# Retention and two expert layers on one core: state products ahead of scores times values, weight sets ahead of conversions, stores begun in the attention

## The chip, the cores and the metric

The kernel runs on one core of a Trainium2 chip. The metric is the device time in microseconds of one execution; of several runs the median counts. The core's engines are TensorE (PE, with its weight loads as PEld), VectorE (DVE), ScalarE (ACT), GpSimd (POOL) and SyncE (SP), which issues nearly all DMAs.

## What is computed

```python
# q, k, v: (4, 8, 768, 64); retention with a decaying state, head by head
for t in range(S):
    state = gamma * state + einsum('bhd,bhe->bhde', k[:, :, t], v[:, :, t])
    y[:, :, t] = scale * einsum('bhd,bhde->bhe', q[:, :, t], state)
x = y.transpose(0, 2, 1, 3).reshape(3072, 512)
h = x @ moe_w_in;  x = maximum(0.01 * h, h) @ moe_w_out     # 512 -> 2048 -> 512
h = x @ moe2_w_in; x = (h - tanh(h)) @ moe2_w_out           # 512 -> 2048 -> 512
```

The weights come as 64-bit floats (two int32 words each) and are made into 32-bit floats on the chip.

## The kernel before

The kernel writes each engine's order out by hand: an instruction stands in its engine's queue where the Python code emits it, and an engine works its queue strictly in order.

**Attention.** The 768 positions are cut into six chunks c of 128, the eight heads into four pairs p. A step s is one (c, p) for all four batches; 24 steps, in the order c = 0, 1 for pair 0, then for pair 1, and so on, so that steps 0, 2, 4, 6 are of chunk 0 and steps 17, 19, 21, 23 of chunk 5. A step runs, on TensorE, the transposes of the next step's k (`a_Tk`, kTp, L515) and of half of a q (`a_Tq`, qTp, L529), the output y (`a_Y`): U times q (L573, not for chunk 0, which has no state yet) and masked scores A times v (L577), then the state product u = k times v (`a_U`, L596, not for chunk 5), then the next step's scores sc (`a_S`, L550). VectorE masks the scores into A (L554) and adds u to the state U (L600); ScalarE scales k (L494), copies kT (L517), qT (L530) and the three pieces of y into x (L581, and L583 twice), and for chunk 0 copies u (L598); GpSimd scales q (L506). SP loads k, q, v for step s + 4 in step s (L447, L458).

**Background work in the attention.** After each step from `CONV_FROM` on, `run` emits some 2.3 us (`ATT_US`) of VectorE work from two queues, taking the second where the first has nothing to give. `conv` is the conversion of the 16 column blocks of moe_w_in: a raw block of 512 KB is loaded (L202, three blocks ahead), then ScalarE does one operation (L208) and VectorE four (L212, L214, L217, L220). `bg` makes what the products need: `build_xc`, the activations of the first two chunks split into a high part on ScalarE (xch, L174) and a low part on VectorE (xcl, L180), with differences between them (L385); and `build_wg(g)`, a weight set from two converted blocks: high parts wg on ScalarE (L174, L176), sums s (L327, L329, L335, L337) and low parts wg (L180, L182) on VectorE. In even steps `bg` comes first, in odd ones `conv`.

**Products.** Behind the attention TensorE runs moe_w_in in a form with seven products (P1 to P7) for each set g and each pair of chunks sb; a product is six matmuls (L768). VectorE adds pairs of results (L781), ScalarE copies (L775) and rectifies (L757), SP stores g1s (L758). The rest of the sets and conversions, and of the activations, is emitted between the products. The first 12 products use sets 0 and 1 alone. In the same place SP stores the 16 outputs x of chunks 2 to 5 to x1s, one behind each product (L829). They are loaded again later as the next activations.

Of the kernel before, what the change touches and what calls it, by code (L numbers as in the profile page):

```python
# [14 lines left out]
AF = mybir.ActivationFunctionType  # L15
# [4 lines left out]
P = 128  # L20
NB, NH, NS, ND = 4, 8, 768, 64
DM, DFF = 512, 2048
NC = NS // P
NPAIR = NH // 2
# [14 lines left out]


N_ATT, N_FFN = 64, 94
CONV_FROM, ATT_US = 5, 2.3

LOAD_LEAD = 5
KV_BUFS = 6
# [29 lines left out]
def kernel(  # L75
# [12 lines left out]
    nc = tc.nc  # L88
# [12 lines left out]
    x1s = dr.tile([NC, NK, P, TB], F32, tag="x1s", name="x1s")  # L101
# [10 lines left out]
    def alloc(nm, dt=F32, shape=(P, TB)):  # L112
        pool, tag = free.popleft()
        serial[0] += 1
        t = pool.tile(list(shape), dt, tag=tag, name=f"{nm}_{serial[0]}")
        home[id(t)] = (t, pool, tag)
        return t

    def give(*ts):
        for t in ts:  # L120
            _, pool, tag = home.pop(id(t))
            free.append((pool, tag))
# [5 lines left out]
    def run(queues, us):  # L128

        while us > 0:  # L130
            for queue in queues:
                cost = next(queue[0], "end") if queue else None
                if cost is not None:
                    break
            if cost is None:
                return 0.0
            if cost == "end":
                queue.popleft()
            else:
                us -= cost  # L140
        return us
# [171 lines left out]
    def build_wg(g):  # L313
        while g + NG not in UN or g not in UN or len(free) < 10:
            yield None
        yield from form_sets(UN.pop(g), UN.pop(g + NG), lambda w, ts: WG.update({g: (w, ts)}))
# [104 lines left out]
            done()  # L421

    xw = {}

    def free_x():
        give(*(xw.pop((c, p)) for c in range(2) for p in range(NPAIR)))


    with tc.tile_pool(name="at", bufs=2, reuse_waits="tile") as at, \
            tc.tile_pool(name="atp", bufs=1, space=PSUM, reuse_waits="tile") as atp:  # L430
        steps = [(c, p) for cc in range(0, NC, 2) for p in range(NPAIR) for c in (cc, cc + 1)]
        S = {}

        def a_load(s):
            if s >= len(steps):
                return
            c, p = steps[s]
            load_kv(s, "k", k)
            if c % 2:
                a_load_q(s + 1)  # L440
            load_kv(s, "v", v)
# [91 lines left out]
        def a_T(s):  # L533
            a_Tk(s)
            if s % 2:
                a_Tq(s + 1, 0)
            else:
                a_Tq(s, 2)

        def a_S(s):  # L540
            if s >= len(steps):
                return
            c, p = steps[s]
            d = S[s]
            tq = slice(c % 2 * P, (c % 2 + 1) * P)
            sc = [atp.tile([P, NB, P], F32, tag=f"sc{h}", name=f"sc_{s}_{h}") for h in range(2)]
            for b in range(NB):
                for h in range(2):
                    r = slice(h * ND, (h + 1) * ND)
                    nc.tensor.matmul(sc[h][:, b, :], d["kT"][r, b, :], d["qT"][r, b, tq], start=True, stop=True)  # L550
            d["A"] = []
            for h in range(2):
                a = at.tile([P, NB, P], F32, tag=f"A{h}", name=f"A_{s}_{h}", bufs=1)
                nc.vector.scalar_tensor_tensor(out=a, in0=sc[h], scalar=_decay(2 * p + h) ** -float(P), in1=tri4,  # L554
                                               op0=ALU.mult, op1=ALU.mult)
                d["A"].append(a)

        def a_Y(s):
            c, p = steps[s]
            d = S[s]  # L560
            tq = slice(c % 2 * P, (c % 2 + 1) * P)
            half = (slice(0, ND), slice(ND, P))
            ys = [atp.tile([P, NB, P], F32, tag=f"y{i}", name=f"y_{s}_{i}") for i in range(2)]

            def place(b, h):
                i = b // 2
                return ys[i][half[h ^ i], b % 2, :]

            if c > 0:
                for b2 in range(2):  # L570
                    for b in (b2, b2 + 2):
                        for h in range(2):
                            nc.tensor.matmul(place(b, h), U[p][half[h], b, :], d["qT"][half[h], b, tq], start=b2 == 0,  # L573
                                             stop=False)
            for b in range(NB):
                for h in range(2):
                    nc.tensor.matmul(place(b, h), d["v"][:, b, h, :], d["A"][h][:, b, :], start=c == 0 and b % 2 == 0,  # L577
                                     stop=b % 2 == 1)
            xw[c, p] = x = alloc("x1")
            flat = [y.rearrange("p b t -> p (b t)")[:, :2 * P] for y in ys]  # L580
            nc.scalar.activation(out=x[:, :2 * P], in_=flat[0], func=AF.Copy)  # L581
            for h in range(2):
                nc.scalar.activation(out=x[half[h], 2 * P:], in_=flat[1][half[1 - h]], func=AF.Copy)  # L583
            if c == 1 and p == NPAIR - 1:
                XQ[0] = {nm: [xw[th, 2 * kh], xw[th, 2 * kh + 1]]
                         for nm, kh, th in (("B11", 0, 0), ("B21", 1, 0), ("B12", 0, 1), ("B22", 1, 1))}

        def a_U(s):
            c, p = steps[s]
            d = S[s]  # L590
            if c < NC - 1:
                u = atp.tile([P, NB, ND], F32, tag="u", name=f"u_{s}")
                for b in range(NB):
                    for h in range(2):
                        r = slice(h * ND, (h + 1) * ND)
                        nc.tensor.matmul(u[r, b, :], d["k"][:, b, h, :], d["v"][:, b, h, :], start=True, stop=True)  # L596
                if c == 0:
                    nc.scalar.activation(out=U[p], in_=u, func=AF.Copy)  # L598
                else:
                    nc.vector.scalar_tensor_tensor(out=U[p], in0=U[p], scalar=gc[:, p:p + 1], in1=u, op0=ALU.mult,  # L600
                                                   op1=ALU.add)
            if c % 2:
                del S[s - 1], S[s]

        conv = deque([conversion(conv_in)])
        bg = deque([build_xc(one, 0, 0), build_wg(0), build_xc(one, 0, 1), build_wg(1), build_xc(one, 0, 2, free_x)])
        us = 0.0
# [12 lines left out]
        for s in range(len(steps)):  # L620
            a_load(s + 4)
            a_scale_k(s + 2)
            if s % 2:
                a_scale_q(s + 3)
            if s == 0:
                a_Tk(1)
                a_Y(0)
                a_Tq(2, 0)
            else:
                a_T(s + 1)  # L630
                a_Y(s)
            a_U(s)
            a_S(s + 1)
            tick[0] += 3
            if s >= CONV_FROM:
                us = run((conv, bg) if s % 2 else (bg, conv), min(us + ATT_US, ATT_US))

# [25 lines left out]
    def upper_g(o):  # L665
        if o < 2 * NT:
            G[o] = alloc("gh", F32R), None
            upper(G[o][0], GR[o])
# [138 lines left out]
    bg.extend(build_wg(g) for g in range(2, NG))  # L807
    bx = deque(build_xc(one, sb, part) for sb in range(1, NSB) for part in range(3))
    loads = deque(load_xq(one, sb, lambda at=SPAN * (sb - 1) + 38: now[0] >= at) for sb in range(1, NSB))
    xleft = [(c, p) for c in range(2, NC) for p in range(NPAIR)]  # L810
    us = 0.0
    for i, (at_, sb, g, nm) in enumerate(stream):
        an, bn, bk, _ = PROD[nm]
        while g not in WG or bn not in XC.get(sb, {}):
            tick[0] += 1
            run((loads, bg, bx, conv), 0.01)
        product(sb, g, nm)
        now[0] = at_
        tick[0] += 1
        done, late[:] = late[:], []  # L820
        used = collect(sb, g, nm)
        for args in done:
            rectify(*args)
        if sb == NSB - 1 and nm == "P4":
            give(*WG[g][1])
        if xleft:
            c, p = xleft.pop(0)
            t = xw.pop((c, p))
            nc.sync.dma_start(out=x1s[c, p], in_=t)  # L829
            give(t)  # L830
        us = run((loads, conv, bg, bx) if not sb and at_ >= BG_FIRST and at_ % 2 == 0 else (loads, bg, bx, conv), min(us + SLOT_US - used, SLOT_US))
        if len(stream) - 11 <= i < len(stream) - 11 + G_AHEAD:
            load_g(i - len(stream) + 11)
        if len(stream) - 6 <= i < len(stream) - 3:
            upper_g(i - len(stream) + 6)
        if len(stream) - 5 <= i < len(stream) - 3:
            lower_g(i - len(stream) + 5)
        if i == len(stream) - 2:
            step(0)
# [71 lines left out]
    us = 0.0  # L911
    for n in range(ND_FROM):
# [16 lines left out]
        us = run((loads, bx, forms, conv), min(us + 2.0, 2.0))  # L929
# [195 lines left out]
    while i < NPROD or halves:  # L1125
# [11 lines left out]
        while halves and (i == NPROD or gone < i * n_mid / NPROD):  # L1137
            o, half = halves[0]
# [9 lines left out]
def _decay(h):  # L1148
    return 1.0 - 2.0 ** (-5.0 - h)
# [49 lines left out]
```

## Time and profile before

| | |
|---|---|
| median of 3 runs | 1058.73 us (1057.42 to 1059.09) |
| profiled execution, its own time | 1059.45 us |
| its span | 1057.7 us |
| PE busy | 1041.5 us (98%) |
| DVE, ACT busy | 826.7 us (78%), 721.1 us (68%) |
| chain that ended last | PE 89%, DVE 4%, DMA 3%, ACT 2% |
| granted TensorE clock | 1.0 of full speed, all through |

The attention takes the first 109 us, the first products follow. Busy time is an average over stages with different limits, so the stages are looked at one by one: which wait ends last there. Matmul ends are modelled, so a small gap of TensorE is seen better in its weight loads (PEld).

### The profile page before, as it was taken

To read this page: it belongs to the slowest core of one execution; us is meant where nothing else is said; L and a number is where in the kernel's file an instruction comes from. 1 tells how busy PE (TensorE), PEld (TensorE's weight loads), DVE (VectorE), ACT (ScalarE), POOL (GpSimd) and SP (SyncE) were. 2 spreads that over 40 slices of the span, in tenths; PEclk is the share of its full clock that TensorE was granted. 3 is DMA by queue.
4 is the path that set the end of the run, shared out by engine and by line. 5 is a ranking of instruction groups with operands and counts; after the bars stand their busy time and mean duration, and the time that the engine had idled before them with its cause. 6 is when DMAs were issued, how large, how long until landed. Compare 5 with 4: busy or idle time off the path is not lost.

```text
span 1057.7 us, 17635 instructions
## 1 busy us (share of the span) xinstructions
PE 1041.5 (98%) x5931; PEld 902.2 (85%) x5931; DVE 826.7 (78%) x1363; ACT 721.1 (68%) x1299; POOL 93.2 (9%) x124
## 2 busy tenths in 40 slices
PE   9999899999999999999999999999999999999998
PEld 6888778888888888888888888888888888888887
DVE  3589897774788999967999789898878988687630
ACT  6889676766776556656777679887668766666440
POOL 3232000000000000000110111001100110011000
PEclk9999999999999999999999999999999999999999
DMA  9998465675668899959999988998987988878641
GB/s 223 242 269 233 164 234 190 208 250 210 225 234 286 287 361 388 393 200 285 276 323 298 324 257 260 303 290 261 316 252 224 268 246 255 259 220 229 190 149 40
DMA packets 208634, 267.67 MB, mean 253 GB/s; under 512 B 65056, under 2 KB 106144, under 8 KB 208544
## 3 DMA queue, kind: packets, MB, share of 16 engines
q1 hardware_dynamic: 197888, 247.52, 70.1%
q0 software_dynamic: 10368, 18.88, 10.3%
q8 instruction: 47, 0.77, 0.3%
q14 instruction: 43, 0.35, 0.1%
q10 hardware_dynamic: 288, 0.15, 0.1%
HBM read 161.63 MB, written 85.98 MB: 234 GB/s over the span
## 4 chain that ended last, share of the span: by engine, by line
PE 89%; DVE 4%; DMA 3%; ACT 2%; issue 1%; SPq 0%; DVEq 0%; ACTq 0%
PE o L693 46%; PE Xd L1040 11%; PE X L768 9%; PE Yd L1040 6%; PE Y L768 4%; PE Zd L1040 3%; PE y L577 2%; PE sc L550 2%; PE Z L768 2%; PE kTp L515 1%; PE y L573 1%; PE qTp L529 1%; DVE c L781 1%; PE u L596 1%; DMA gr<-g1s 1%
## 5 line engine op out<-in xcount | busy, mean ns | idle before, releaser
L693 PE MATMUL o<-gh,wo 128*128 128x512 f32 x768 | 239.5, 379 | 0.0
L693 PEld LDWEIGHTS o<-gh,wo 128*128 128x128 f32 x768 | 145.2, 189 | 20.4
L174 ACT ACTIVATE gh<-gr 128x512 fp32r<-128x512 f32 x192 | 118.3, 621 | 54.1 <-DMA gr<-g1s 26.9
L180 DVE TENSOR_TENSOR gl<-gr,gh 128x512 fp32r<-128x512 f32 x192 | 130.1, 683 | 27.9 <-ACT gh L174 22.5
L693 PE MATMUL o<-gl,wo 128*128 128x512 f32 x384 | 145.9, 380 | 2.5 <-DVE gl L180 2.5
L693 PE MATMUL o<-w2h,gh 128*128 128x512 f32 x384 | 145.5, 379 | 0.0
L693 PE MATMUL o<-w2h,gl 128*128 128x512 f32 x384 | 145.5, 379 | 0.0
L693 PE MATMUL o<-w2l,gh 128*128 128x512 f32 x384 | 145.5, 379 | 0.0
L1020 POOL DMA_DIRECT2D et<-h x72 | 62.1, 862 | 826.9 <-DVE gl L180 424.3
L1040 PE MATMUL Xd<-xch,wf 128*128 128x512 f32 x384 | 129.5, 379 | 0.0
L768 PE MATMUL X<-xch,wg 128*128 128x512 f32 x384 | 123.2, 381 | 3.7 <-DVE wg L180 2.5
L1007 DVE COPY_PREDICATED es<-mk,et 128x512 f32<-128x512 uint16 x96 | 70.9, 742 | 44.6 <-ACT mk L981 44.6
L768 PEld LDWEIGHTS X<-xch,wg 128*128 128x128 f32 x384 | 72.4, 189 | 17.0 <-DVE wg L180 3.4
L693 PEld LDWEIGHTS o<-gl,wo 128*128 128x128 f32 x384 | 72.6, 189 | 14.3 <-DVE gl L180 4.1
L969 ACT ACTIVATE eu<-h 128x512 f32<-128x512 f32 x96 | 59.9, 624 | 33.3 <-DVE h L949 31.2
L693 PEld LDWEIGHTS o<-w2l,gh 128*128 128x128 f32 x384 | 72.6, 189 | 10.3
L693 PEld LDWEIGHTS o<-w2h,gh 128*128 128x128 f32 x384 | 72.6, 189 | 10.3
L1040 PEld LDWEIGHTS Xd<-xch,wf 128*128 128x128 f32 x384 | 72.6, 189 | 10.3
L693 PEld LDWEIGHTS o<-w2h,gl 128*128 128x128 f32 x384 | 72.6, 189 | 10.3
L1040 PE MATMUL Xd<-xcl,wf 128*128 128x512 f32 x192 | 72.8, 379 | 0.0
L768 PE MATMUL X<-xcl,wg 128*128 128x512 f32 x192 | 72.8, 379 | 0.0
L985 DVE SCALAR_TENSOR_TENSOR ew<-eu,h 128x512 f32<-128x512 f32 x96 | 65.5, 683 | 8.8 <-DMA wfs<-wg 3.2
(101 smaller groups left out, 2030.3 us busy)
## 6 DMA issues: line engine op xcount, KB each, us to landing
wf<-wfs SPq DMA_DIRECT2D x168, 256.0 KB, 4.3
g1s<-c SPq DMA_DIRECT2D x96, 256.0 KB, 2.2
gr<-g1s SPq DMA_DIRECT2D x96, 256.0 KB, 5.3
g2s<-es SPq DMA_DIRECT2D x96, 256.0 KB, 3.5
gr<-g2s SPq DMA_DIRECT2D x96, 256.0 KB, 4.2
et<-h POOLq DMA_DIRECT2D x72, 256.0 KB, 5.3
raw<-in_moe_w_in_dram SPq DMA_DIRECT2D x32, 512.0 KB, 5.7
raw<-in_moe_w_out_dram SPq DMA_DIRECT2D x32, 512.0 KB, 4.4
```

What stands on the lines that cost most here:

```text
L174: nc.scalar.activation(out=hi, in_=src, func=AF.Copy)
L180: nc.vector.tensor_tensor(out=lo, in0=src, in1=hi.bitcast(F32), op=ALU.subtract)
L515: nc.tensor.transpose(ps[:, b, :], d["k"][:, b].rearrange("p h d -> p (h d)"), ident)
L550: nc.tensor.matmul(sc[h][:, b, :], d["kT"][r, b, :], d["qT"][r, b, tq], start=True, stop=True)
L577: nc.tensor.matmul(place(b, h), d["v"][:, b, h, :], d["A"][h][:, b, :], start=c == 0 and b % 2 == 0, stop=b % 2 == 1)
L693: nc.tensor.matmul(ACC[j], a, il(b), start=first and i == 0, stop=last and i == 2)
L768: nc.tensor.matmul(ps, w[:, c], il(x), start=first and kt == 0 and i == 0, stop=kt == 1 and i == 2, skip_group_check=True)
L969: nc.scalar.activation(out=e["u"], in_=h, func=AF.Square)
L985: nc.vector.scalar_tensor_tensor(out=e["w"], in0=e["u"], scalar=C3, in1=h, op0=ALU.mult, op1=ALU.mult)
L1007: nc.vector.copy_predicated(out=e["s"], mask=e["mk"].bitcast(mybir.dt.uint16), data=e["th"])
L1020: nc.gpsimd.dma_start(out=e["th"], in_=h, accum_op=ALU.add)
L1040: nc.tensor.matmul(ps, a, il(b), start=nm in ("P1", "P2", "P5") and kt == 0 and j == 0, stop=kt == 1 and j == 2, skip_group_check=True)
```

## The change

It does five things. (1) `a_U` moves from behind `a_Y` into it: the state product u is emitted behind U times q and ahead of A times v (behind the transposes, where U times q is missing). (2) In steps 0 to 7 (`DVE_UNTIL` = 8) the two half copies of y are VectorE's. (3) Background work begins after step 2 instead of step 5. (4) `bg` comes first in every step. (5) From step 16 (`STORE_FROM`) on, each step stores one x, and the products the rest; `store_x` is the old code in a function.

```diff
-CONV_FROM, ATT_US = 5, 2.3
+CONV_FROM, ATT_US = 2, 2.3
+STORE_FROM, DVE_UNTIL = 16, 8
...
+    xleft = [(c, p) for c in range(2, NC) for p in range(NPAIR)]
+
+    def store_x():
+        if xleft:
+            c, p = xleft.pop(0)
+            t = xw.pop((c, p))
+            nc.sync.dma_start(out=x1s[c, p], in_=t)
+            give(t)
...
                             nc.tensor.matmul(place(b, h), U[p][half[h], b, :], d["qT"][half[h], b, tq], start=b2 == 0,
                                              stop=False)
+            a_U(s)
             for b in range(NB):
...
             for h in range(2):
-                nc.scalar.activation(out=x[half[h], 2 * P:], in_=flat[1][half[1 - h]], func=AF.Copy)
+                if s < DVE_UNTIL:
+                    nc.vector.tensor_copy(x[half[h], 2 * P:], flat[1][half[1 - h]])
+                else:
+                    nc.scalar.activation(out=x[half[h], 2 * P:], in_=flat[1][half[1 - h]], func=AF.Copy)
+            if c % 2:
+                del S[s - 1], S[s]
...
-            a_U(s)
             a_S(s + 1)
+            if s >= STORE_FROM:
+                store_x()
             tick[0] += 3
             if s >= CONV_FROM:
-                us = run((conv, bg) if s % 2 else (bg, conv), min(us + ATT_US, ATT_US))
+                us = run((bg, conv), min(us + ATT_US, ATT_US))
...
-        if xleft:
-            c, p = xleft.pop(0)
-            t = xw.pop((c, p))
-            nc.sync.dma_start(out=x1s[c, p], in_=t)
-            give(t)
+        store_x()
```

The emission follows the queues, so the order moves as well. VectorE, from the last A of the attention on (wg, xcl, s as above; cv is a block in conversion, c an addition of two products), before:

```order
L554 SCALAR_TENSOR_TENSOR A_1_1860<-sc_1_1849,cst 128x512
L180 TENSOR_TENSOR wg_1800<-cv_895,wg_1799 128x512
L335 TENSOR_TENSOR s_58_1798<-cv_895,cv_1048 128x256
L337 TENSOR_TENSOR s_58_1798<-cv_895,s_57_1797 128x256
L180 TENSOR_TENSOR wg_1802<-s_57_1797,wg_1801 128x512
L180 TENSOR_TENSOR wg_1804<-s_58_1798,wg_1803 128x512
L781 TENSOR_TENSOR c_1917<-Z_0_1910,P_68_1903 128x512
L182 SCALAR_TENSOR_TENSOR wg_1805<-cv_1048,wg_1805 128x256
L180 TENSOR_TENSOR xcl_1922<-x_6_557,xch_1921 128x512
```

and of the change (its lines are shifted: L563 is L554, L213 L212, L221 L220, L328 L327, L795 L781):

```order
L563 SCALAR_TENSOR_TENSOR A_1_1887<-sc_1_1876,cst 128x512
L213 TENSOR_SCALAR cv_1776<-cv_1776 128x512
L215 TENSOR_SCALAR cv_1776<-cv_1776 128x512
L218 SCALAR_TENSOR_TENSOR cv_1776<-raw_0_1236,cv_1776 128x512
L221 SCALAR_TENSOR_TENSOR cv_1776<-raw_0_1236,cv_1776 128x512
L213 TENSOR_SCALAR cv_1890<-cv_1890 128x512
L215 TENSOR_SCALAR cv_1890<-cv_1890 128x512
L218 SCALAR_TENSOR_TENSOR cv_1890<-raw_0_1774,cv_1890 128x512
L221 SCALAR_TENSOR_TENSOR cv_1890<-raw_0_1774,cv_1890 128x512
L328 TENSOR_TENSOR s_81_1945<-cv_1238 128x256
L330 TENSOR_TENSOR s_81_1945<-s_81_1945,cv_1001 128x256
L795 TENSOR_TENSOR c_1966<-Z_0_1959,P_80_1942 128x512
```

Before, the rest of weight set 1, six xcl and four differences still stand behind the last A, and eight of the 16 conversions of moe_w_in are done ahead of it. With the change none of these stands there, both sets and all activations of the first two chunks are made ahead of it, and six conversions are.

SP, around the first raw loads (k_591 is the k of step 10), before:

```order
L447 DMA k_510<-in_k_dram 128x4x64 x2
L458 DMA q_513<-in_q_dram 128x4x128 x2
L447 DMA v_516<-in_v_dram 128x4x64 x2
L202 DMA raw_0_585<-in_moe_w_in_dram 128x4x256
L202 DMA raw_0_587<-in_moe_w_in_dram 128x4x256
L202 DMA raw_0_589<-in_moe_w_in_dram 128x4x256
L447 DMA k_591<-in_k_dram 128x4x64 x2
L447 DMA v_594<-in_v_dram 128x4x64 x2
```

and of the change, where k_315 is that of step 6 and k_381 that of step 7:

```order
L456 DMA k_315<-in_k_dram 128x4x64 x2
L456 DMA v_318<-in_v_dram 128x4x64 x2
L203 DMA raw_0_375<-in_moe_w_in_dram 128x4x256
L203 DMA raw_0_377<-in_moe_w_in_dram 128x4x256
L203 DMA raw_0_379<-in_moe_w_in_dram 128x4x256
L456 DMA k_381<-in_k_dram 128x4x64 x2
L467 DMA q_384<-in_q_dram 128x4x128 x2
L456 DMA v_387<-in_v_dram 128x4x64 x2
```

The raw loads move ahead by three steps of k, q and v. Up to the last v of the attention SP then issues seven raw loads and three x1s stores, where it issued nine raw loads and no store.

ScalarE between two kT, in step 16 (chunk 4), before:

```order
L517 ACTIVATE kT_1389<-kTp_1384 128x512
L530 ACTIVATE qT_1391<-qTp_0_1392 128x2x2x128
L581 ACTIVATE x_44_1416<-y_0_1398 128x256
L583 ACTIVATE x_44_1416<-y_1_1399 64x256 x2
L174 ACTIVATE wg_1134<-s_30_1130 128x512
L208 ACTIVATE cv_1450<-raw_0_1293 128x512
L494 ACTIVATE k_1295<-k_1295,lead 128x4x64 x2
L517 ACTIVATE kT_1475<-kTp_1470 128x512
```

and of the change (L596 is L583, L175 L174, L177 L176):

```order
L526 ACTIVATE kT_1423<-kTp_1418 128x512
L539 ACTIVATE qT_1425<-qTp_0_1426 128x2x2x128
L591 ACTIVATE x_57_1460<-y_0_1432 128x256
L596 ACTIVATE x_57_1460<-y_1_1433 64x256 x2
L175 ACTIVATE wg_1323<-s_48_1318 128x512
L177 ACTIVATE wg_1325<-cv_830 128x256
L175 ACTIVATE xch_1484<-x_8_581 128x512
L175 ACTIVATE xch_1486<-x_11_726 128x512
L503 ACTIVATE k_1330<-k_1330,lead 128x4x64 x2
L526 ACTIVATE kT_1512<-kTp_1507 128x512
```

Two pieces of background work between y and the next kT have become four.

## Rows read from the trace of the kernel before

**Rows 1.** Attention, first products: PE, PEld, DVE, ACT, POOL busy (instructions); clock, DMA share, GB/s

```profile
13.00:109.00 96.00, 94.57 (x1548) 81.42 (x1548) 69.20 (x118) 81.20 (x182) 26.91 (x40) 1.00 0.92 236
109.00:165.00 56.00, 50.97 (x233) 42.50 (x230) 50.95 (x97) 40.29 (x73) 0.00 (x0) 1.00 0.55 197
```

**Rows 2.** Who TensorE waited for, 104 to 165 us: total, times, longest

```profile
PE X L768 <- DVE wg L180: 2.5, 2, 1.3
PE Y L768 <- DVE xcl L180: 1.7, 1, 1.7
...
PE Y L768 <- DVE wg L180: 0.4, 1, 0.4
```

**Rows 3.** VectorE by line and shape, 109 to 165 us: busy, mean ns, idle before

```profile
L180 DVE TENSOR_TENSOR wg<-s,wg 128x512 fp32r<-128x512 f32 x10 | 6.6, 693 | 2.8 <-ACT wg L174 2.8
...
L217 DVE SCALAR_TENSOR_TENSOR cv<-raw,cv 128x512 int32<-128x512 int32 x8 | 6.5, 807 | 0.2
...
L180 DVE TENSOR_TENSOR xcl<-x,xch 128x512 fp32r<-128x512 f32 x6 | 3.9, 684 | 1.5 <-ACT xch L174 1.5
...
L214 DVE TENSOR_SCALAR cv<-cv 128x512 int32<-128x512 int32 x8 | 3.4, 424 | 0.2
...
L385 DVE TENSOR_TENSOR x<-x,x 128x512 f32<-128x512 f32 x4 | 2.6, 682 | 0.0
...
L335 DVE TENSOR_TENSOR s<-cv,cv 128x256 f32<-128x256 f32 x5 | 2.1, 416 | 0.0
```

**Rows 4.** Two VectorE operations of 512 columns in a row

```profile
117.09 1.28 DVE L385 TENSOR_TENSOR x<-x,x 128x512 f32<-128x512 f32 x2
```

**Rows 5.** TensorE's weight loads in time order, steps 4 and 5: start, us, [idle]

```profile
28.56 0.74 PEld L577 LDWEIGHTS y<-A,v 128*64 128x64 f32 x13 [0.23 <-DVE A L554]
...
30.04 0.97 PEld L550 LDWEIGHTS sc<-qT,kT 64*128 64x128 f32 x16
...
34.24 0.97 PEld L550 LDWEIGHTS sc<-qT,kT 64*128 64x128 f32 x16
```

**Rows 6.** The same, the two steps in which TensorE waited for kT

```profile
47.04 0.97 PEld L550 LDWEIGHTS sc<-qT,kT 64*128 64x128 f32 x16 [0.45 <-ACT kT L517]
...
52.11 1.06 PEld L550 LDWEIGHTS sc<-qT,kT 64*128 64x128 f32 x16 [0.94 <-ACT kT L517]
```

**Rows 7.** ScalarE in time order: one early step, then the two steps of rows 6

```profile
30.77 0.90 ACT L494 ACTIVATE k<-k,lead 128x256 f32<-128x256 f32 x2
...
45.54 0.96 ACT L494 ACTIVATE k<-k,lead 128x256 f32<-128x256 f32 x2 [1.10 <-DMA k<-in_k_dram]
...
47.39 0.38 ACT L581 ACTIVATE x<-y 128x256 f32<-128x256 f32 x1
...
48.59 2.19 ACT L174 ACTIVATE xch<-x 128x512 fp32r<-128x512 f32 x4
...
51.48 0.57 ACT L517 ACTIVATE kT<-kTp 128x512 f32<-128x512 f32 x1
```

**Rows 8.** The first three raw loads: issue, and time to landing

```profile
L202 SPq DMA_DIRECT2D raw<-in_moe_w_in_dram x3: 617/694/722, 36.6 to 38.1; - x3
...
DMA to landing us min/median/max: 5.7/6.4/7.0
```

**Rows 9.** The k load right behind them

```profile
L447 SPq DMA_DIRECT2D k<-in_k_dram x2: 442/1062/1683, 38.8 to 39.3; - x2
...
DMA to landing us min/median/max: 6.7/6.7/6.7
```

**Rows 10.** The k load of step 7, with no raw ahead of it

```profile
L447 SPq DMA_DIRECT2D k<-in_k_dram x2: 440/472/505, 25.3 to 25.8; - x2
...
DMA to landing us min/median/max: 2.8/2.8/2.8
```

**Rows 11.** VectorE by line and shape in the attention, 13 to 109 us

```profile
L554 DVE SCALAR_TENSOR_TENSOR A<-sc,cst 128x512 f32<-128x512 f32 x46 | 29.6, 684 | 18.0 <-PE sc L550 17.9
L600 DVE SCALAR_TENSOR_TENSOR U<-U,lead,u 128x256 f32<-128x256 f32 x16 | 7.6, 475 | 9.6 <-PE u L596 9.6
```

More of the change, by code (lines that the diff above doesn't have):

```diff
@@ L601, in a_U @@
                                                    op1=ALU.add)
-            if c % 2:
-                del S[s - 1], S[s]
         conv = deque([conversion(conv_in)])
@@ L809 @@
     loads = deque(load_xq(one, sb, lambda at=SPAN * (sb - 1) + 38: now[0] >= at) for sb in range(1, NSB))
-    xleft = [(c, p) for c in range(2, NC) for p in range(NPAIR)]
     us = 0.0
```

## Prediction

> **What bounds the kernel now.** I read the windows by stage first, then who waits for whom on TensorE, then the engines it waits for. TensorE computes 94.57 of 96 us in the attention [rows 1], so a change gains there only through the order of its steps or a stall taken out. In the 56 us behind it TensorE loses 5.03 us while VectorE is busy 50.95 [rows 1]: VectorE is the bound there. The waits name the places [rows 2]: 2.5 + 0.4 us for weight sets (wg) and 1.7 us for one low part of the converted activations (xcl). These 4.6 us are the largest loss that the change can reach.
>
> In the attention the reader is to see three things. A step of the first chunk, which has no state-times-query products, waits 0.23 us for the masked scores A [rows 5]. Two steps wait 0.45 and 0.94 us for kT [rows 6]. And the reason for these is on ScalarE [rows 7]: it sat 1.10 us until a k load had landed, and in the next step it had four xch conversions (2.19 us) ahead of its next kT.
>
> **Products stage.** The order shows what leaves it. Behind the last A there were six xcl, four x differences (L385) and six operations of weight set 1; now there are none of these, but ten conversions instead of eight. By the durations [rows 3]: 6 x 0.684 + 4 x 0.682 + 3 x 0.693 + 3 x 0.416 = 10.2 us go; a conversion is 0.42 + 0.42 + 0.81 + 0.81 = 2.5 us (L220 taken like L217, L212 like L214), so two more cost 4.9. VectorE is relieved of 5.2 us.
>
> Does TensorE get it? A product is six matmuls of 50.97 / 233 = 0.219 us [rows 1], 1.31 us. Sets 0 and 1 carry the first 12 products, 15.7 us. Until set 2 is complete VectorE has two conversions (4.9), two additions (1.4), five 256-column and three 512-column operations (4.2): 10.5 us by durations. But operations in a row overlap: two of 0.68 take 1.28 [rows 4], one each 0.60, so 88%: 9.3 us, and 6.4 us of lead. Each later set comes every 7 products (9.2 us) and costs VectorE two conversions, one set and three additions: 4.9 + 4.2 + 2.0 = 11.1 us by durations, 9.8 with the overlap. Five sets eat 3.0 of the 6.4 us. So the wg and xcl waits go and I take **-4.6 us**. Bounds: -5.0 (all that TensorE loses there goes) and -1.7 (only the xcl wait goes, for that work is no longer there; the wg waits return, as they would by the durations without overlap, since 5 x 1.9 is more than 5.2).
>
> **States before values.** u moves between U-times-q and A-times-v; it adds no instruction and its inputs k and v have landed steps before. Where U-times-q is missing (steps 0, 2, 4, 6), u fills the 0.23 us for A [rows 5]: 4 x 0.23 = **-0.9 us**, between that and nothing. The other steps have the same products in another order: nothing. The price is that ScalarE's copies of y now start as the scores start, no longer behind u as well; that shortens the time that ScalarE has from one y to the next kT, see the last term.
>
> **Half of the copies to VectorE, steps 0 to 7.** 16 copies. The nearest row is U, also 256 columns from PSUM, 0.475 us [rows 11], 7.6 us in all. VectorE waited 17.9 us for scores and 9.6 us for u in the attention [rows 11], mostly in these steps; that hides them. Without this cover, in the two steps that also hold a conversion, A would come some 0.5 us late, and u in front of A-times-v gives that back. ScalarE loses the same copies. Taken as nothing, at most 1.0 the wrong way.
>
> **Conversion from step 2.** The first three raw loads now stand on SP ahead of the k of step 7 instead of step 10. This removes and adds a stall. Removed: the late k and, as the four xch now follow a step with one ScalarE copy less and no late k, the wait behind them: 0.45 + 0.94 [rows 6], **-1.4 us**. Added: the old k behind the raws was issued 2.2 us after the first of them and took 6.7 us [rows 8, 9]; k of step 7 took 2.8 from 25.3 us [rows 10]. Shifted by 2.2 + 3.9 it lands at 34.2; as SP's queue is emptier there, I take one us less, 33.2. ScalarE scaled it at 30.77 [rows 7]. TensorE's scores follow the scaling by 1.5 us (45.54 to 47.04, [rows 6, 7]), so 34.7; they stood at 34.24 [rows 5] and would stand at 33.55 with three shorter steps. That is 1.2 us, and the k of step 8 still some 0.7 late: **+1.9 us**. Bounds: 0.4, as before, and 4.2, all three raws at the 1.4 us between their landings (first 36.6 + 5.7, last 38.1 + 7.0, two between [rows 8]).
>
> How long the debt lasts decides much. The DMA engines show a share of 0.92 at 236 GB/s in the attention [rows 1]; read as room, that is a twelfth, and a debt of 4.2 us would last some 50 us (rival 2). The Trainium skill ("DMA: Bandwidth & Descriptors", section "Where 436 GB/s comes from") puts the limit of transfers from HBM at about 358 GB/s per core; by it 122 GB/s would be spare and the three raws (1.57 MB) caught up within an estimated 13 us, three steps. The trace before shows no stretch at that rate. I keep the sum at two late k because only one k came late behind the raws before [rows 7].
>
> **Weight sets ahead of conversion.** ScalarE's pieces pile up where they are not alternated: behind step 16 the order has four (two wg, two xch), at 2.19 / 4 = 0.55 us [rows 7] some 2.0 us, and the step that follows has no u. ScalarE is idle (96 - 81.2) / 24 = 0.62 us a step [rows 1]. So between nothing and 1.4 us; I take **+0.6 us**, nearer to the low end because k and kT come before qT.
>
> **Stores.** Eight of the 16 x1s stores go out from step 16 on, three of them ahead of the last loads, where the seven raws ahead of the last v were nine. Half a raw each, 0.7 us of the queue: 2.1 against 2.8 saved. Taken as nothing.
>
> **Sum.** -4.6 - 0.9 - 1.4 + 1.9 + 0.6 = -4.4 us. The profiled execution took 1059.45 us (span 1057.7 and 1.75 around it): 1055.05. The median of the runs is 0.72 below it, so I predict **1054.3 us**. With all terms at their good ends -5.0 - 0.9 - 1.4 + 0.4 = -6.9, at their bad ends -1.7 - 1.4 + 4.2 + 1.4 + 1.0 = +3.5.
>
> **Rival 1, the weight sets wait again.** VectorE works in order; its lead is spent while it waits for the product that an addition needs, and ten conversions remain. Then only the xcl wait goes: 2.9 us less gain, 1057.2 us. For it: without overlap sets 5 to 7 are late. Against: VectorE idles 5 us in that stage today, partly for ScalarE [rows 3], and set 2 now has 6 us of lead.
>
> **Rival 2, slower: the loads pace the attention.** If SP never regains the lead that the early raws cost, each transfer ahead of the last v delays the attention: seven raws at 1.4 and three stores at 0.7 are 11.9 us. -4.6 - 0.9 - 1.4 + 11.9 + 0.6 = +5.6: 1064.3 us. It decides from the point where k lands later than ScalarE wants it in step after step, beyond step 9. For it: the share of 0.92. Against: nine raws before cost 1.4 us of waiting only, and the k behind three of them came just 1.10 us late [rows 7].
>
> **How the numbers follow.** A measurement of this kernel tells 0.2% (2.1 us) from no change, so faster is below 1056.6. My forecast has a chance of 0.74 (1051.5 to 1056.6, from the good ends), rival 1 0.16 (no change), rival 2 0.10 (slower). The range leaves out rival 2 and the edges of the others: 1051.5 to 1057.6.
>
> **What would show it.** Right: no wait of TensorE for xcl or wg between the end of the attention and 165 us; a first product still near 109 us; ScalarE waiting some 2 to 3 us for the k of steps 7 and 8, and none later; step 16 half a us longer. Wrong: k waits beyond step 9, or wg waits over 1 us in all, or a gain that stands elsewhere than before 165 us.

## The result and the profile after

The change makes the kernel slower: 1064.96 us, the median of six runs (1064.46 to 1067.85), against 1058.72 us before (six runs), a ratio of 1.0066 with a 95% interval of 1.0053 to 1.0079. I had predicted 1054.3 us, so the forecast missed by 10.7 us and had the wrong sign. The profiled execution is the slowest of the six: 1067.85 us, span 1066.1 us. It stands 2.9 us above the median, and its terms below add up to more than the median shows.

The attention and the first products, in windows that meet near the first product, as in [rows 1] (same columns):

```profile
13.00:111.00 98.00, 94.25 (x1529) 79.30 (x1529) 78.88 (x142) 77.66 (x173) 26.36 (x40) 0.98 0.93 245
111.00:165.00 54.00, 53.53 (x255) 46.46 (x251) 49.97 (x94) 37.46 (x69) 0.00 (x0) 1.00 0.56 191
```

Who TensorE waited for (total, times, longest), from 104 to 165 us, where [rows 2] stood:

```profile
PE Y L782 <- ACT P L789: 0.5, 1, 0.5
PE y L587 <- DMA raw<-in_moe_w_in_dram: 0.2, 1, 0.2
PE y L587 <- DVE A L563: 0.2, 1, 0.2
```

and from 165 to 300 us, where the kernel before has one entry, 0.7 us for c:

```profile
PE Y L782 <- DVE xcl L181: 1.0, 4, 0.3
PE X L782 <- ACT xch L175: 0.9, 2, 0.4
PE X L782 <- DVE xcl L181: 0.8, 3, 0.3
PE X L782 <- DVE c L795: 0.7, 2, 0.3
PE Y L782 <- ACT xch L175: 0.5, 1, 0.5
PE Z L782 <- DVE xcl L181: 0.2, 1, 0.2
```

The reader is to see that the products do what was forecast: the waits for weight sets and for the first xcl are gone, and TensorE loses 0.5 us between 111 and 165 us. But waits of a kind that the profile before did not have stand behind 165 us, for the activations of the next chunks (xch, xcl). The clock of the attention is 0.98 of full speed; before, it was 1.00.

The sizes come from comparing the start of the same matmul in both traces, after minus before. Behind the first layer four more names occur: gl is the low part of a loaded result of the first layer, st a copy of finished output, kp ScalarE's copy of a product of the second layer, wf a weight set of the second layer as TensorE uses it.

| place | time before | change minus before | what happened since the line above |
|---|---|---|---|
| first product | 109.23 us | +2.26 us | attention |
| products, first pair of chunks, late | 161.97 | -3.67 | -5.9: no wait for wg, xcl |
| second pair of chunks, after its start | 203.50 | +0.13 | +3.8: xch, xcl |
| third pair, after its start | 276.64 | +2.53 | +2.4: xch, xcl |
| products with moe_w_out begin | 354.08 | +2.78 | +0.25 |
| moe_w_out and second layer mixed | 521.35 | -0.01 | -2.8: two gl waits of before (1.76 and 0.74 us) are not paid here |
| the same | 561.60 | +4.04 | +4.0: its own waits for st and gl |
| the same | 609.30 | +8.16 | +4.1: kp, st |

So the gain of the products was real, and it was gone by 203 us. That is where the experiments look.

### The profile page after: what moved, and what is told of

It is laid out like the page before. It is cut to its first block, busy times and chain, and to the rows that moved or that the text cites. A ratio compares the mean times of both kernels' runs of the same rounds, so it can differ in the third digit from the quotient of the medians.

```text
span 1066.1 us, 17641 instructions
## 1 busy us (share of the span) xinstructions
PE 1043.5 (98%) x5931; PEld 900.4 (84%) x5931; DVE 832.6 (78%) x1379; ACT 710.9 (67%) x1283; POOL 92.7 (9%) x124
## 4 chain that ended last, share of the span: by engine, by line
PE 88%; DVE 4%; DMA 4%; ACT 3%; issue 2%; SPq 0%; ACTq 0%; DVEq 0%; POOLq 0%; POOL 0%
PE o L707 44%; PE Xd L1049 11%; PE X L782 10%; PE Y L782 5%; PE Yd L1049 5%; PE Z L782 3%; PE Zd L1049 2%; PE sc L559 2%; PE y L587 2%; PE kTp L524 1%; DMA gr<-g1s 1%; PE u L611 1%; PE y L582 1%; PE qTp L538 1%; DVE xcl L181 1%
## 5 line engine op out<-in xcount | busy, mean ns | idle before, releaser
L175 ACT ACTIVATE gh<-gr 128x512 fp32r<-128x512 f32 x192 | 118.4, 623 | 62.3 <-DMA gr<-g1s 22.1
L1002 DVE SCALAR_TENSOR_TENSOR es<-es,ew 128x512 f32<-128x512 f32 x96 | 66.1, 688 | 4.0
```

The lines of the kernel that those rows point to most:

```text
L175: nc.scalar.activation(out=hi, in_=src, func=AF.Copy)
L1002: nc.vector.scalar_tensor_tensor(out=e["s"], in0=e["s"], scalar=K1, in1=e["w"], op0=ALU.add, op1=ALU.mult)
```

## The experiments

Each kernel was timed together with the kernel before on the same chip. The kernel before took 1060.4 us beside the kernels with later loads, with the old alternation, with the raws one a step from step 2 and with the states alone; 1060.0 us beside the repeat, the released loads, the start at step 5 and the copies on ScalarE; and 1059.9 us beside the two that combine edits. So ratios are given; the times in the expectations were written against 1058.7 us, in the two that combine edits against 1059.5. xq_B names the loads of the next activations from x1s, g1s the results that the products store.

**The changed kernel again** (no edit).

> The changed kernel itself, run again, for what of its profile repeats. If the losses belong to its order of work: a wait of about 2 us for the k of step 7 at 33 us, waits for xch and xcl at 184 and 262 us, a wait behind wf near 610 us; time 1064 to 1069 us. If the wait near 610 us was chance (the profiled execution was 2.9 us above the median), it is missing in this profile.

Measured: 1066.0 us, ratio 1.0058 (1.0046 to 1.0070). Its own profile, span 1063.2 us, repeats the structure: waits for xch and xcl at 182 to 191 and 261 to 266 us, and the one near 610 us, which is therefore not chance:

```profile
610.34 0.80 PE L1049 MATMUL Xd<-xch,wf 128*128 128x512 f32 x1 [3.02 <-ACT kp L951]
```

What does not repeat is the size of the wait for the k of step 7. It was 1.99 us in the first profile and 0.90 here, and the first products start 0.53 us later than before instead of 2.26. The load of q, which stands behind the raws as well, is late too, so that TensorE waits for the scaled q (qp):

```profile
33.84 1.23 PE L559 MATMUL sc<-qT,kT 64*128 64x128 f32 x16 [0.90 <-ACT kT L526]
36.35 1.01 PE L538 MATMUL qTp<-cst,qp 128*128 128x128 f32 x4 [0.69 <-POOL qp L515]
```

Two kernels below keep these loads as they are. With the activation loads released the wait at this place was 0.42 us and the first products started 1.00 us earlier than before; with all copies on ScalarE it was 2.21 us and they started 2.21 us later. One profile therefore says little about what an edit does to this stall.

**The kernel before with later loads of the activations.**

```diff
-    loads = deque(load_xq(one, sb, lambda at=SPAN * (sb - 1) + 38: now[0] >= at) for sb in range(1, NSB))
+    loads = deque(load_xq(one, sb, lambda at=SPAN * (sb - 1) + 42: now[0] >= at) for sb in range(1, NSB))
```

> The kernel before, with the loads of the next activations (xq_B) allowed four products later (42 instead of 38 products into each pair of chunks) and nothing else changed. Theory 1 (late loads of activations cost the changed kernel 3.8 + 2.4 us): waits of TensorE for xch and xcl appear at the start of the second and third pair of chunks, 2.5 to 4 us each, none before 165 us; the same gap opens in the second expert layer only if its order moves too. Total 1058.7 + 5 to 7 = 1064 to 1066 us. Theory 2 (the activations were late only because the products ran 3.4 us ahead of them): in the kernel before the products are not ahead, so at most 1 us each: under 1061 us.

Measured: 1073.19 us, ratio 1.0122 (1.0104 to 1.0141), about 13 us. With nothing of the change in it, the waits of the changed kernel appear between 165 and 300 us:

```profile
PE Y L768 <- DVE xcl L180: 1.5, 6, 0.3
PE Y L768 <- ACT xch L174: 1.0, 2, 0.5
PE X L768 <- ACT xch L174: 0.9, 2, 0.4
```

The same matmul stands 4.0 us further behind over the second pair and 3.9 us over the third, and near 606 us 4.6 us more is lost behind kp and 1.7 us at half the clock (1.2 GHz) behind that wait. Theory 2, that only the lead of the products made the activations late, falls. Its own profile also lost 2.7 us to late loads in an attention that is the same code as before, a difference between executions of the size that the repeat above shows.

**The changed kernel with the activation loads released.** In the code a load of activations is held until no conversion is under way (`raws`). This edit lifts that for the first layer.

```diff
-        while not may() or raws[0]:
+        while not may() or (raws[0] and side is not one):
```

> The changed kernel with the loads of the next activations of the first expert layer no longer held back until the last conversion in progress is done: the first is issued behind the 19th store of g1s, as in the kernel before, instead of the 22nd. Theory 1 (what is lost behind 165 us comes from the late loads): attention and products as in the changed kernel (first products 2.3 us later than before, 165 us reached 3.7 us earlier), but the waits for xch and xcl at 184 and 262 us shrink from 3.8 + 2.4 us to under 2 us in all, and no wait for kp or wf near 610 us: 1064.96 - 4 to 8 = 1057 to 1061 us. Theory 2 (ScalarE and VectorE make the activations too late, whenever they are loaded): the same waits, 1064 us or more.

Measured: 1056.29 us, ratio 0.9965 (0.9953 to 0.9977). Against the changed kernel on the same chip this is 9.7 us less, for one condition. The profiles put it behind the attention: from 162 us to the end the repeat of the changed kernel falls back by 10.7 us against the kernel before, this one by 0.9. ScalarE in time order, its first activation pieces, of the changed kernel:

```profile
180.94 1.66 ACT L175 ACTIVATE xch<-xq_B 128x512 fp32r<-128x512 f32 x3
183.12 0.63 ACT L175 ACTIVATE xch<-xq_B 128x512 fp32r<-128x512 f32 x1 [0.52 <-DMA g1s<-c]
185.32 1.23 ACT L175 ACTIVATE xch<-xq_B 128x512 fp32r<-128x512 f32 x2
```

and with the loads released:

```profile
171.97 2.21 ACT L175 ACTIVATE xch<-xq_B 128x512 fp32r<-128x512 f32 x4
178.10 1.13 ACT L175 ACTIVATE xch<-xq_B 128x512 fp32r<-128x512 f32 x2
```

The place among the products says the same without times. The second pair of chunks needs these pieces from product 56 on (7 products for each of 8 sets). In the kernel before, the first of them runs behind 48.7 products (292 product matmuls by six), in the changed kernel behind 53.0 (318), and with the loads released behind 48.7 again. The first load itself goes out behind 38.5, 41.5 and 37.5 products. With the loads released, TensorE waited from 165 to 300 us for this alone:

```profile
PE X L782 <- DVE c L795: 0.7, 2, 0.4
```

The loss near 610 us went too. Its cause is seen on SP, which stores the last of eight weight sets of the second layer (wfs), seven stores in a row. In the changed kernel:

```profile
599.49 0.32 SPq L895 DMA_DIRECT2D wf<-wfs  x1
599.86 4.33 SPq L305 DMA_DIRECT2D wfs<-wg  x6
604.23 1.29 SPq L307 DMA_DIRECT2D wfs<-wg  x1
605.62 1.20 SPq L677 DMA_DIRECT2D gr<-g1s  x1
606.91 1.13 SPq L895 DMA_DIRECT2D wf<-wfs  x1
```

and with the loads released:

```profile
478.04 3.97 SPq L305 DMA_DIRECT2D wfs<-wg  x6
482.11 0.61 SPq L307 DMA_DIRECT2D wfs<-wg  x1
```

The gr load behind them goes out at 605.62 us, and ScalarE, which works in order, waits for it with the kp that TensorE needs behind it:

```profile
610.84 0.63 ACT L175 ACTIVATE gh<-gr 128x512 fp32r<-128x512 f32 x1 [4.35 <-DMA gr<-g1s]
...
613.03 0.58 ACT L951 ACTIVATE kp<-Xd 128x512 f32<-128x512 f32 x1
```

The set is stored 122 us later than with the loads released (599.86 against 478.04), and 116 us later than before (483.5). It slips in every kernel in which the first activation load goes out behind 39.8 products or more (the changed kernel and its repeat 41.5, copies on ScalarE 41.7, before with later loads 41.8, start at step 5 39.8), and in none of the seven others, at 37.5 to 38.5. Moving the loads alone moves the set both ways (later loads in the kernel before, released loads in the changed kernel and in the one from step 5 on); the steps between the two were not followed.

**The changed kernel with the old alternation of the queues.**

```diff
-                us = run((bg, conv), min(us + ATT_US, ATT_US))
+                us = run((conv, bg) if s % 2 else (bg, conv), min(us + ATT_US, ATT_US))
```

> The changed kernel with the old alternation of the two background queues (conversions first in odd steps). Ten conversions then stand ahead of the last A instead of six, and the loads of the next activations are issued behind the 19th store of g1s, as in the kernel before, instead of the 22nd. Theory 1: the attention still pays for the late k of step 7 (scores of that step 2 us late, then the clock at half speed), products start near 111; the waits for xch and xcl at 184 to 193 and 262 to 268 us are gone (3.8 + 2.4 us): 1064.96 - 6.2 = 1058.8 us. Theory 2 (VectorE's total work sets the pace): the waits move into weight sets before 165 us and the time stays near 1065 us.

Measured: 1070.56 us, ratio 1.0091 (1.0076 to 1.0105). Neither theory had this. Ten conversions are ahead of the last A, the activation loads come in time and no wait stands at 184, 262 or 610 us; but the attention ends 5.8 us later than before, and the products lose up to 9 us more to what was not made ahead of them (5.9 of these are left at the end of the first pair). Three of the waits were followed by half the clock, at 103, 124 and 151 us. TensorE's waits over the whole run:

```profile
PE sc L559 <- ACT kT L526: 6.7, 7, 2.4
PE X L782 <- DVE wg L181: 4.1, 2, 2.4
PE Y L782 <- ACT xch L175: 2.8, 1, 2.8
```

So with the start at step 2, sets first is the better order. One more k comes late here, and TensorE waits 1.97 us behind it at 100 us; in SP's queue a raw load and a store of x1s stand right ahead of it. That it is late by these is not shown.

**The changed kernel with its first three raw loads one a step.**

```diff
         for n in range(ahead):
             load(n)
+            start = tick[0] + gap
+            while tick[0] < start:
+                yield None
...
-        conv = deque([conversion(conv_in)])
+        conv = deque([conversion(conv_in, gap=3)])
```

> The changed kernel with its first three raw loads issued one a step (steps 2, 3, 4), each between the loads of two steps, instead of all three in a row ahead of the k of step 7. Theory 1: the stall of 2.0 us at 33 us and the half clock behind it (1.6 us) go or shrink below 0.5 us, so the first products start near 108; seven conversions stand ahead of the last A, the activation loads stand behind the 19th store again, and the waits at 184 and 262 us go too: 1064.96 - 3.4 - 6.2 = 1055.4 us. Theory 2 (the loads pace the attention, only their sum counts): the k of later steps are late instead, the products start at 111 as in the changed kernel, and the time is 1059 us or more.

Measured: 1056.53 us, ratio 0.9960 (0.9945 to 0.9975), 3.8 us below before where theory 1 had 3.3. The stall at the k of step 7 is not in its profile. TensorE in the changed kernel:

```profile
31.89 1.05 PE L587 MATMUL y<-A,v 128*64 128x128 f32 x16
34.93 1.75 PE L559 MATMUL sc<-qT,kT 64*128 64x128 f32 x16 [1.99 <-ACT kT L526]
36.60 1.12 PE L524 MATMUL kTp<-cst,k 128*128 128x128 f32 x4
```

and with the loads spread:

```profile
32.24 1.04 PE L590 MATMUL y<-A,v 128*64 128x128 f32 x16
33.22 1.16 PE L562 MATMUL sc<-qT,kT 64*128 64x128 f32 x16
34.31 0.66 PE L527 MATMUL kTp<-cst,k 128*128 128x128 f32 x4
```

This kernel paces its background work differently as well: the first activation load goes out behind 37.5 products, and neither the waits at 184 and 262 us nor the late set appear. That is most of its gain, and the spreading is not told from it: its first products start at 108.81 us, while the changed kernel's attention, with the raws in a row, gave 111.48, 109.75 and 108.23 us in three profiles, and the kernel with the loads released is as fast (ratio 0.9965). What it still loses is a wait of 1.22 us for a weight set at 153 us and one of 2.97 us for gl at 490 us, shortly behind the seven stores of the last set (from 478.9 us).

**The changed kernel with the background from step 5 on.**

```diff
-CONV_FROM, ATT_US = 2, 2.3
+CONV_FROM, ATT_US = 5, 2.3
```

> The changed kernel with the background work beginning behind step 5 again, not step 2; all else as changed. Theory 1: no late k in step 7 (the raws stand ahead of the k of step 10 again, 0.5 to 1.3 us late there), so the first products start 2 to 3 us earlier than in the changed kernel, 108.5 to 109.5; only five conversions stand ahead of the last A, so the loads of the next activations are still one to two products later than before and half of the 6.2 us of waits for xch and xcl stays: 1064.96 - 2.5 - 3 = 1059.5 us (1057 to 1062). Theory 2 (starting early is what pays for the products): weight sets wait again, 3 us or more, and the time is 1063 us or more.

Measured: 1056.28 us, ratio 0.9965 (0.9952 to 0.9977), 3.7 us below before and better than either theory. The first products start 0.98 us earlier than before. TensorE is 7.35 us ahead at 159 us and does not wait for activations (load behind 39.8 products, first piece behind 50.2). But the last set is late (stored at 589.07 us), and the lead shrinks from 10.4 us at 521 us to 2.1 at 609: by 3.0 us in two waits for gl up to 554 us, and by 5.2 us near 603 us, in a wait of 3.43 us for kp and at half the clock behind it. Five conversions ahead of the last A, fewer than the six of the changed kernel, thus put the loads earlier (39.8 for 41.5).

**Both: from step 5 on, loads released.**

> The changed kernel with both of the last two edits: background work from step 5 on again, and the loads of the next activations not held back. Theory 1 (the early start and the late loads are what the change loses by): attention as with the start at step 5 alone (first products near 108.2), 7.4 us ahead of before at 165 us, the eighth weight set of the second layer stored near 480 us instead of 589, no wait for wf or kp near 600 us; a wait for gl of 2 to 3 us near 490 us, as in the kernel with the released loads. 1059.5 - 7.4 + 1.5 = 1053.6 us (1051 to 1055.5). Theory 2 (that one eighth set comes late with every start at step 5): 1056.3 us as with the start at step 5 alone.

Measured: 1055.90 us, ratio 0.9959 (0.9945 to 0.9973). The last set is stored at 478.96 us again and nothing is lost near 600 us, but 1.3 us is lost to a late c at 179 us, and TensorE waits 2.59 us for gl at 491 us, where the kernel before waits 1.76. That is 4.0 us below before, where theory 1 had 5.9 and at least 4.0, and it is not told from the kernels with one of the two edits. In the profile, other waits took part of what the last set gave.

**The same with the raws one a step.**

> As the kernel before this one, with the first three raw loads issued one a step from step 5 on. Theory 1: the late k of step 10 (1.06 us of idle TensorE at 45.4 us) goes as well: first products near 107.3, 1 us faster than the kernel with the raws in a row: 1052.6 us. Theory 2 (each raw then delays one later k by as much): first products near 108.2 and the same time.

Measured: 1057.54 us, ratio 0.9978 (0.9967 to 0.9989), by the medians 1.6 us slower than without the spreading. In its profile the late k of step 10 goes (the scores 4.20 us apart instead of 5.42), and later steps pay (5.54, 5.36 and 5.17 us at 72, 82 and 99 us; first products at 110.25); waits of 0.76, 1.90 and 0.34 us between 157 and 183 us follow in the products. Here theory 2 is nearer. Spreading the raws gave nothing that these runs show by itself.

**States before values, alone.** The changed kernel with four of its five parts undone.

```diff
-CONV_FROM, ATT_US = 2, 2.3
-STORE_FROM, DVE_UNTIL = 16, 8
+CONV_FROM, ATT_US = 5, 2.3
+STORE_FROM, DVE_UNTIL = 99, 0
...
-                us = run((bg, conv), min(us + ATT_US, ATT_US))
+                us = run((conv, bg) if s % 2 else (bg, conv), min(us + ATT_US, ATT_US))
```

> The kernel before with one part of the change alone: the state products u ahead of scores times values; conversions from step 5 on, old alternation, all copies of y on ScalarE, no stores in the attention. Theory 1 (the ledger of the two profiles): the four steps of chunk 0 are each 0.4 us shorter (4.02 to 3.61 us between scores), so the first products start 1.6 to 1.8 us earlier, near 107.5; the products of moe_w_in and the loads of the next activations stay at the same product numbers, so that all of it reaches the end: about 1057.0 us. Theory 2 (VectorE's work up to the second pair of chunks sets the pace): the first products start 1.7 us earlier, but TensorE waits that much longer for weight sets: 1058.7 us, no change.

Measured: 1058.86 us, ratio 0.9989 (0.9979 to 0.9998), 1.2 us with an interval of 0.2 to 2.2: nearer to the 1.7 us of theory 1 than to none, and only just clear of none. Three steps of chunk 0 are 0.41 us shorter (4.02 to 3.61 us between scores) and the first 0.31. In the profile most of this hides, for the k of step 10 is 0.9 us later in that execution.

**All copies on ScalarE.**

```diff
-STORE_FROM, DVE_UNTIL = 16, 8
+STORE_FROM, DVE_UNTIL = 16, 0
```

> The changed kernel with all copies of y on ScalarE (none on VectorE); the order of everything else is the same. If these copies were hidden on either engine, as I took them: within 1 us of the changed kernel in the same runs, the first products at the same time. If VectorE was short in steps 0 to 7: 1 to 2 us faster. If ScalarE needs the relief: the scores of steps 1 to 8 wait for kT, 1 to 3 us slower.

Measured: 1066.85 us, ratio 1.0065 (1.0045 to 1.0085), against 1066.0 for the changed kernel on the same chip. Its first products start at 111.43 us, those of the changed kernel at 111.48 and 109.75 in its two profiles. Where these copies run makes no difference that is told here.

The stores in the attention were not tried alone: the sets made early use the tiles that these stores give back.

## Why the prediction was wrong

**The step that failed** is what I made of "ten conversions instead of eight" behind the last A: 4.9 us of VectorE inside a relief of 5.2 us, and nothing further. I read the order of the changed kernel only up to 165 us and gave what lies behind no term at all. What I did not follow is that the loads of the next activations are held until the last conversion of moe_w_in is through. In the changed kernel these loads go out 3.0 and 4.0 products later (behind 41.5 for 38.5 and 97.8 for 93.8), the activations are late for 3.8 + 2.4 us, and the last set of the second layer slips by 116 us. Shown: releasing the loads alone gives 9.7 us, delaying them alone in the kernel before costs 13 us. With them released the change gains 3.7 us, near the 4.4 of my sum, though not term by term.

Why the conversions are through later is not their number alone: with five ahead of the last A (start at step 5) the loads stood earlier than with six. The durations and the relief were right. The kernel emits background work in portions of 1.3 us for each product (`SLOT_US`), and beyond that in a loop that runs whenever a weight set or an activation is not made yet when its product is to be emitted. Added up from the costs that the code gives its own operations, the work emitted behind the attention until the last conversion is through falls from 45.0 to 39.7 us, much as forecast. But 10.9 us of the 45.0 were emitted by that loop, and only 0.4 us of the 39.7, for the sets are now ready. In portions the work rises from 34.1 to 39.3 us: the conversions are emitted through behind 41 products instead of 35 (VectorE starts the last operation of the last one behind 39.2 instead of 36.5). The loads are allowed from product 38 on, so the kernel before had some slack there and the changed kernel has none. So the lateness of the sets, which the change removed, had also pushed the conversions forward.

**Products stage, -4.6 us:** right in kind; -5.9 up to the end of that stage, in all three profiles of this order (changed kernel, repeat, loads released), beyond the good end of -5.0. The idle time of [rows 2] went, and each wait that went gave 0.27 us beyond the idle time shown (1.95 for the 1.69 of xcl, 1.60 for the 1.33 of the first wg).

**States before values, -0.9 us:** right in kind, too small. A step of chunk 0 gains 0.41 us, not 0.23: the wait for A [rows 5] goes, and 0.18 us beyond it. One cost was missed. With u ahead of A times v, u is sooner at the buffer that VectorE's U must have read. At 73 us U is late, and u waits:

```profile
73.35 0.69 PE L611 MATMUL u<-v,k 128*64 128x64 f32 x16 [0.37 <-DVE U L615]
```

With a wait for A behind it that step is 0.8 us longer than before (5.36 us for 4.54); in the repeat it took 4.52.

**Late k of steps 7 and 8, +1.9 us:** the mechanism and the place were right, and the scores of 34.93 us were forecast at 34.7. That the size fits is partly luck: in the other profiles of this attention the scores stand at 33.84 and 33.20 us. The k of step 8 was not late for TensorE. What I did not have is the clock and the late q: behind the wait of 1.99 us TensorE worked at half speed (1.2 GHz) for 3.4 us, and the next step took 5.17 us instead of 3.61. In the repeat, at full clock, that step took 4.94 us, with the wait of 0.69 us for qp shown above; so the 1.6 us are not the clock's alone. Three windows in the columns of [rows 1], the first right behind the raw loads, the others behind the wait:

```profile
27.00:30.00 3.00, 3.00 (x53) 2.54 (x52) 1.52 (x4) 2.80 (x7) 0.00 (x0) 1.00 1.01 346
...
35.00:37.00 2.00, 2.00 (x18) 1.78 (x19) 0.29 (x1) 1.50 (x4) 1.55 (x3) 0.58 1.06 239
37.00:39.00 2.00, 2.00 (x20) 1.67 (x20) 1.93 (x5) 1.65 (x4) 0.79 (x2) 0.56 0.91 208
```

**How long the debt of the raws lasts** was the question of rival 2. The DMA engines moved 346 GB/s for 3 us behind the raws, well above the mean of 236 [rows 1], and from 41 to 87 us TensorE waited no more than 0.3 us for any kT. So the mean was not the limit. By the limit of about 358 GB/s that the Trainium skill gives ("DMA: Bandwidth & Descriptors", section "Where 436 GB/s comes from") the debt was an estimated 13 us. The traces do not agree with that limit: the engines moved 367 GB/s from 28 to 31 us in the changed kernel, and 410 GB/s from 439 to 442 us in the kernel before, whose trace I had wrongly said to show no stretch at that rate. What the trace shows of the debt is that two steps behind the wait the scores stand 4.20 us apart again (40.09, 44.30 and 48.50 us). Rival 2 gave 1064.3 us, close to the measured time, but by a mechanism that did not happen: that is luck.

**Stalls removed, -1.4 us:** -0.9 (the steps of 4.58 and 5.07 us became 4.20 and 4.55). **Step 16, +0.6 us:** not seen; steps 16 and 17 take 4.20 us as before, but the step at 88 us lost 0.49 us to kT. **Copies, stores, 0:** the copies as taken; the stores were not separated.

**Sum.** Attention +2.26 in the profiled execution where I had +0.2, and +0.53 in the second; products -5.9 for -4.6; behind them nothing forecast, and +11.8 us in the profiled execution (from -3.67 to +8.16), +10.7 in the second. The good ends, -6.9 us, give 1051.8 us and not the 1051.5 of the range.

## What to carry to other kernels

Where a hand-made planner emits work in portions, follow its order until the plan of before and after meet again, and count the portions as well as the engine's microseconds. Work that a planner emits because something is late moves other work forward too; when a change removes the lateness, that other work can end later. A loader that waits for the end of a queue then turns this into late data several stages on. Ahead of such a change, look in the order for the due places (here product 56 and the eighth set) and see how much slack stands before each. And after a large expected gain that did not show, find the place where the two traces meet again; here 203 us pointed to the cause.

## What the runs showed of the hardware

The granted clock of TensorE fell to half behind some of the longer waits and not behind others. Over all profiles here, from 13 to 1045 us, it fell behind waits of 1.97, 1.99, 2.06, 2.21, 2.39, 2.82, 2.97, 3.03, 3.43 and 4.29 us; it did not fall behind 2.15, 2.23, 2.38, 2.59, 2.64 and 2.77 us, nor behind any shorter than 1.97. The longest stretch at half clock was behind the 2.97 us (gl at 490 us, loads spread), where the clock was 0.53 for 6 us:

```profile
490.00:494.00 4.00, 1.03 (x5) 0.86 0.76 259
494.00:500.00 6.00, 6.00 (x15) 0.53 0.63 211
```

There the half clock cost 2.8 us on top of the wait, over the same matmuls; near 603 to 621 us, behind the waits for kp (repeat, start at step 5, later loads), it cost 1.5 to 1.7 us.

VectorE's operations that read only SBUF were longer while GpSimd scaled q. Rows of GpSimd and then of VectorE, changed kernel:

```profile
68.72 3.64 POOL L515 TENSOR_TENSOR qp<-q,lead 128x256 f32<-128x256 f32 x4 [5.04 <-DMA q<-in_q_dram]
```

```profile
70.02 0.83 DVE L183 SCALAR_TENSOR_TENSOR wg<-cv,wg 128x256 fp32r<-128x256 f32 x1
70.78 2.12 DVE L386 TENSOR_TENSOR x<-x,x 128x512 f32<-128x512 f32 x2
72.83 0.47 DVE L615 SCALAR_TENSOR_TENSOR U<-U,lead,u 128x256 f32<-128x256 f32 x1
73.22 1.27 DVE L563 SCALAR_TENSOR_TENSOR A<-sc,cst 128x512 f32<-128x512 f32 x2
```

Two differences took 2.12 us where they take 1.28 alone [rows 4], and the wg piece of 256 columns 0.83 us, where it takes 0.41 in the attention without GpSimd. U and A of these rows ran behind GpSimd's end, at 72.36 us. Over all profiles, in the attention, 100 A and 57 U ran wholly while GpSimd worked, and took 0.69 and 0.47 us as always; they read PSUM. Conversion operations with a single operand (cv from cv) took 0.75 us for 0.42. Behind the long differences U came late at 73 us.

Executions of one kernel differ by more in these runs than in the three of before at the start: 1052.8 to 1058.7 us for the kernel with both edits, and 1057.9 to 1063.4 us for the kernel before beside it. The profiles show one place of it: loads in the attention make TensorE wait for the same k by 0.4, 0.9 and 2.0 us in three executions.
